# Induced attention and an ELU feed-forward: the first block attended token-major, the first batch's projected weights written in place, the first block's second layer unsplit in plain fp32, and a new order of the opening

## The chip, the cores and the metric

The kernel runs on one core of a Trainium2 chip. The metric is device time in microseconds (us); the time of a kernel is the median of its runs. The kernel before took 1676.34 us (three runs: 1674.83, 1676.34, 1676.71).

A core has five engines, each with its own instruction stream that is worked off in order: TensorE (PE in the profile; PEld is its weight load, which overlaps it), VectorE (DVE), ScalarE (ACT), GpSimd (POOL) and SyncE (SP), which here issues all DMAs. They wait for each other through semaphores. SBUF and PSUM have 128 partitions; PE writes to PSUM, in banks of 512 fp32 per partition.

## The reference

```python
def mab(q, kv):                                  # scale = 1/sqrt(128)
    s = scale * (q @ kv.transpose(0, 2, 1))
    s = s - s.max(-1, keepdims=True)
    a = np.exp(s)
    a /= a.sum(-1, keepdims=True) + 1e-09
    return a @ kv
h = mab(I, x)            # 32 inducing points attend over N tokens
y = mab(x, h)            # every token attends over the 32 rows of h
...
h = y @ w_in             # (49920, 128) @ (128, 2048)
g = np.where(h > 0.0, h, np.exp(np.minimum(h, 0.0)) - 1.0)
return g @ w_out         # (2048, 128)
```

`x` is 4 batches of 12480 tokens of 128 features, fp32. The weights arrive as fp64 and are made fp32 on the chip from their two 32-bit words.

## The kernel before

The output of the attention is never formed. For a batch, `h` (32 x 128) is multiplied by `w_in` once (`hw`, 32 x 2048), and the first layer of a block of tokens is `hw` times the softmaxed scores of the tokens. Both factors are split into two parts of the matmul's fast format fp32r, a high one and a rest; `hw` has the rows high, low, high and a row group of ones, a block's `stk` the scores high, high, low and a constant 1/32, so that one fp32r matmul of 128 rows gives the product to fp32 accuracy, plus 1.

A batch is 25 blocks (`BLOCKS`) of 512 or 480 tokens, in 7 groups (`GROUPING`). A block is worked in 8 units (`units`), a unit is 2 chunks of 128 of the 2048 hidden features. Unit n runs `ffn_in` (two matmuls into a PSUM tile `ph`, L638; exp on ACT, L646), `ffn_mid` (max and min on DVE, L652), `ffn_split` (`gh`, the part in fp32r, on ACT, L660), `ffn_low` (the rest `gl`, on POOL or DVE) and `ffn_out` (the second layer into `po`, L723). `PLAN` says how a pair of chunks does the second layer: P and D split it (six fp32r matmuls: `gh` by `wo_h`, `gh` by `wo_l`, `gl` by `wo_h`; the rest on POOL for P, on DVE for D), N does it unsplit with two fp32 matmuls, `e` by `wo_n`. P and N carry a summand of 1 in `g`, which `sum_excess` makes up for: it sums the rows of their weights on PE (L689), and L732 subtracts the sum from the output.

PE runs the second layer of a unit 3 to 5 units behind its first (`RAMP`, `LAG`). `ps_h` has 3 PSUM tiles of two banks, which the units' `ph` and, during the opening, all other products take in turn (`bank`); `ps_o` has two banks for `po`.

The opening, before unit 0, is the first batch's attention of the 32 points over its 12480 tokens (`first_batch`) and the making of the weights. Its order is written by hand in `FIRST`; a name is a step and a number: x, y the transposes of a group's tokens on PE with their copies (`COPIES` gives them to ACT or DVE), s, m scores and their maxima, b the softmax's bias of a phase, w, e, g, h the weights, their transposes, the gather on PE and its sum on DVE, then sum, share, norm, spread (`hT`, the transposed `h`), project and stack (`hw`), room (`hw`'s ones), l0 to l3 the attention of block 0 alone (`attend(b, -1)`), a0 to a3 that of the other three blocks of group 0; A to E with 0 to 3 the four parts of `w_in`, with 4 to 7 those of `w_out`: A takes the words apart (L180, L184), B makes the scale, C and D put a part together (L204, L208, L214 on DVE, L218 on POOL), E splits a part of `w_out` into `wo_h` (L253) and `wo_l` (L254) or copies it to `wo_n` (L251). A step u<n> stands for unit n: steps behind it in `FIRST` are issued after the unit's first layer. `LOADS` is the order of the loads: pieces 0 to 13 of `x`, i0 and i1 the halves of `w_in`; the parts of `w_out` follow. `BY_SCALAR` lists the parts whose scale is made mostly by ACT.

PE, DVE and ACT keep the order in which the code is written (`manual_schedule`); POOL and SP are ordered by a scheduler.

In `project_h` the four quarters of `hw` go side by side into the four partition groups of one bank, a copy and a subtraction split them, and `stack_h` places them with 12 DMAs of 32x512. The attention of block 0 (lone) computes its scores with 4 copies of `h`, transposes the 128x512 scores on DVE (L561), finds maximum, difference, exp, sum and quotient there and on ACT, transposes back (L599) and splits (L602, L604). Later batches are worked in beside the units (`side`, with the due times of `first_half` and `attend`).

Of the kernel before, what the change touches and what calls it, by code (L numbers as in the profile page):

```python
# [48 lines left out]
def kernel(  # L49
# [447 lines left out]
    def room_for_h(b):  # L497

        hw = hwp.tile([P, F], F32R, tag="hw", name=f"hw_{b}")
        if steady:  # L500
            nc.gpsimd.memset(hw[3 * Q :, :].bitcast(F32), 1.0)
# [37 lines left out]
    def lone(b, g):  # L539
        return g < 0  # L540

    def attend_scores(b, g):
# [4 lines left out]
        np_ = P if lone(b, g) else len(blocks) * Q
        ps = bank(f"ps_t_{b}_{g}")
        for j, k in enumerate(blocks):
            n = np_ // len(blocks)  # L550
            nc.tensor.matmul(  # L551
                ps[j * n : (j + 1) * n, :T],
                state[b]["hT4"][:, :n],
                block_xT(b, k),
                start=True,
                stop=True,
            )
# [37 lines left out]
    def attend_stack(b, g):  # L595
# [4 lines left out]
        if lone(b, g):  # L600
            t = home(b, 0)
            nc.scalar.copy(t[: 3 * Q], aT[: 3 * Q])  # L602
# [1 line left out]
            nc.vector.tensor_sub(low, aT[2 * Q : 3 * Q], low.bitcast(F32))  # L604
            return
# [50 lines left out]
    def ffn_split(n):  # L656
        v, how = live[n], plan(n)
        if how != "N":
            v["gh"] = ghp.tile(list(v["e"].shape), F32R, tag="gh", name=f"gh_{n}")
            nc.scalar.activation(v["gh"], v["g"], AF.Copy, bias=-1.0 if how == "D" else 0.0)  # L660
# [14 lines left out]
    def sum_excess():  # L675
        ones = ep.tile([P, TM], F32, tag="e", name="ones")[:, :P]
        ones_r = ones.bitcast(F32R)
        nc.gpsimd.memset(ones, 1.0)
        parts = []
        for cp in range(NCP):  # L680
            f = 2 * cp
            if PLAN[cp] == "P":
                i = WHERE_S[f]
                parts += [(ones_r, wo_h[:, i : i + 2, :]), (ones_r, wo_l[:, i : i + 2, :])]
            if PLAN[cp] == "N":
                parts.append((ones, wo_n[:, WHERE_N[f] : WHERE_N[f] + 2, :]))
        ps = bank("ps_excess")[:, : 2 * C]
        for i, (one, w) in enumerate(parts):
            nc.tensor.matmul(  # L689
                ps, one, w.rearrange("p c d -> p (c d)"),  # L690
                start=i == 0, stop=i == len(parts) - 1,
            )
        for dq in range(4):
            rows = slice(dq * Q, (dq + 1) * Q)
            nc.vector.tensor_reduce(
                out=excess[rows],
                in_=ps.rearrange("p (c d) -> p d c", d=C)[rows, rows, :],
                axis=AX.X, op=ALU.add,
            )
# [239 lines left out]
```

## Time and profile before

| | |
|---|---|
| median of 3 runs | 1676.34 us |
| the profiled execution | 1677.49 us |
| its span, first to last instruction | 1675.7 us |
| instructions in it | 23394 |
| mean granted TensorE clock | 0.987 |
| HBM read / written | 48.94 MB / 25.56 MB |
| first first-layer matmul (`ph`, L638) starts | 66.07 us |
| second layer of unit 8 (the first of block 1) starts | 101.89 us |

The timeline of the profile lists instructions with their start and duration in us, the engine, the line, what they write and read, a count where equal ones are merged, and in brackets how long the engine stood idle before and what ended that. An fp32 matmul shows as two passes: two of them are "x4". The granted clock of TensorE is 1.00 at full speed and 0.50 at half.

### The profile page before, as it was taken

What the parts mean: (1) busy time and instruction counts of PE and PEld (TensorE: products, weight loads), DVE (VectorE), ACT (ScalarE), POOL (GpSimd) and SP (SyncE); (2) the same over time, 40 slices, a digit from 0 to 9 for tenths busy, and PEclk for the clock granted to TensorE, in tenths of its full rate; (3) what the DMA queues carried; (4) which work ended last, traced back from release to release, by engine and by line L of the source; (5) the groups of instructions that cost most, each with busy time, mean ns of one, the idle gap of its engine ahead of it and who ended that gap; (6) DMA issues with size and microseconds to landing.
All of it is one profiled execution on the core that took longest, in us unless ns stands there. A gap on an engine that the chain in (4) does not pass through costs nothing.

```text
span 1675.7 us, 23394 instructions
## 1 busy us (share of the span) xinstructions
PE 1624.8 (97%) x7660; PEld 1214.5 (72%) x7660; DVE 1412.2 (84%) x1471; ACT 1483.1 (89%) x1718; POOL 1408.5 (84%) x740
## 2 busy tenths in 40 slices
PE   6699999999999999999999999999999999999998
PEld 4366777777776777777777677777778777777786
DVE  4898888888888888888888988888888888888886
ACT  5588999899898988988889899899889999999996
POOL 3488898887898888988888888888889989998997
PEclk9699999999999999999999999999999999999999
DMA  8253223323224243322323422321221211111111
GB/s 254 48 97 65 63 47 72 73 39 78 65 50 82 39 85 64 58 48 60 87 51 56 76 63 43 77 56 28 68 55 34 38 19 33 34 37 19 31 28 24
DMA packets 384762, 98.18 MB, mean 59 GB/s; under 512 B 364864, under 2 KB 370784, under 8 KB 384384
## 3 DMA queue, kind: packets, MB, share of 16 engines
q1 hardware_dynamic: 384640, 96.68, 28.4%
q8 instruction: 61, 1.00, 0.3%
q14 instruction: 61, 0.50, 0.1%
HBM read 48.94 MB, written 25.56 MB: 44 GB/s over the span
## 4 chain that ended last, share of the span: by engine, by line
PE 73%; DVE 9%; ACT 8%; issue 6%; DMA 2%; POOL 2%; SPq 0%; POOLq 0%; DVEq 0%; ACTq 0%
PE po L723 51%; PE ph L638 18%; ACT e L646 4%; ACT gh L660 3%; DVE e L652 3%; DMA xm<-in_x_dram 2%; PE ps_t L551 1%; DVE gl L669 1%; DVE xT L274 1%; PE ps_hh L418 1%; DVE ph L652 1%; POOL gl L673 1%; PE ps_s L327 1%; DMA out_dram<-o 1%; DVE o L731 0%
## 5 line engine op out<-in xcount | busy, mean ns | idle before, releaser
L673 POOL TENSOR_TENSOR gl<-e,gh 128x1024 fp32r<-128x1024 f32 (+1 forms) x500 | 1169.8, 2357 | 201.4 <-ACT gh L660 190.2
L646 ACT ACTIVATE e<-ph 128x1024 f32<-128x1024 f32 (+1 forms) x800 | 800.9, 1003 | 116.5 <-PE ph L638 114.9
L652 DVE SCALAR_TENSOR_TENSOR e<-ph,e 128x1024 f32<-128x1024 f32 (+1 forms) x600 | 714.3, 1192 | 184.7 <-ACT e L646 178.1
L638 PE MATMUL ph<-stk,hw 128*128 128x512 f32 (+1 forms) x1600 | 540.2, 419 | 16.2 <-DVE e L652 10.1
L723 PE MATMUL po<-gh,wo_h 128*128 128x512 f32 (+1 forms) x1400 | 546.6, 390 | 4.7 <-DVE s L561 2.5
L723 PE MATMUL po<-gh,wo_l 128*128 128x512 f32 (+1 forms) x1400 | 546.7, 390 | 0.3 <-POOL wo_l L254 0.3
L660 ACT ACTIVATE gh<-e 128x1024 fp32r<-128x1024 f32 (+1 forms) x500 | 518.8, 1038 | 25.1 <-DVE e L652 22.8
L723 PE MATMUL po<-gl,wo_h 128*128 128x512 f32 (+1 forms) x1400 | 432.0, 389 | 0.4 <-POOL gl L673 0.4
L638 PEld LDWEIGHTS ph<-stk,hw 128*128 128x128 f32 x1600 | 294.4, 189 | 164.0 <-issue 59.5
L723 PEld LDWEIGHTS po<-gh,wo_h 128*128 128x128 f32 x1400 | 263.4, 188 | 61.5 <-issue 8.2
L723 PEld LDWEIGHTS po<-gl,wo_h 128*128 128x128 f32 x1400 | 263.5, 188 | 58.5 <-POOL gl L673 1.1
L723 PEld LDWEIGHTS po<-gh,wo_l 128*128 128x128 f32 x1400 | 263.4, 188 | 53.6 <-POOL wo_l L254 0.8
L652 DVE SCALAR_TENSOR_TENSOR ph<-ph,e 128x1024 f32<-128x1024 f32 (+1 forms) x200 | 239.5, 1197 | 30.4 <-ACT e L646 28.7
L669 DVE SCALAR_TENSOR_TENSOR gl<-ph,gh 128x1024 fp32r<-128x1024 f32 (+1 forms) x200 | 237.3, 1186 | 0.1
L660 ACT ACTIVATE gh<-ph 128x1024 fp32r<-128x1024 f32 (+1 forms) x200 | 201.2, 1006 | 4.6 <-DVE ph L652 4.2
L723 PE MATMUL po<-e,wo_n 128*128 128x512 f32 (+1 forms) x400 | 183.8, 582 | 0.0
L732 POOL TENSOR_TENSOR o<-o,excess 128x512 f32<-128x512 f32 (+1 forms) x100 | 126.7, 1267 | 3.1 <-DVE o L731 3.1
L723 PEld LDWEIGHTS po<-e,wo_n 128*128 128x128 f32 x400 | 75.2, 189 | 53.2 <-issue 45.9
L731 DVE STREAM_TRANSPOSE o<-po 128x512 f32<-128x512 f32 (+1 forms) x100 | 69.1, 691 | 4.9 <-PE po L723 4.9
L274 DVE STREAM_TRANSPOSE xT<-xq 128x1024 f32<-128x1024 f32 (+2 forms) x39 | 45.5, 1166 | 0.0
L611 POOL TENSOR_TENSOR alo<-aT,ahi 128x512 fp32r<-128x512 f32 (+3 forms) x27 | 34.4, 1275 | 0.8 <-ACT ahi L609 0.8
L418 PE MATMUL ps_hh<-xm,e 128*32 128x128 f32 (+2 forms) x872 | 33.6, 295 | 0.7 <-DVE h L435 0.6
(108 smaller groups left out, 530.3 us busy)
## 6 DMA issues: line engine op xcount, KB each, us to landing
xm<-in_x_dram SPq DMA_DIRECT2D x32, 512.0 KB, 4.7
out_dram<-o SPq DMA_DIRECT2D x240, 64.0 KB, 2.0
xq<-in_x_dram SPq DMA_DIRECT2D x84, 128.0 KB, 3.0
out_dram<-o SPq DMA_DIRECT2D x160, 60.0 KB, 1.9
stk<-ahi SPq DMA_DIRECT2D x118, 64.0 KB, 2.0
xq<-in_x_dram SPq DMA_DIRECT2D x60, 120.0 KB, 2.8
stk<-ahi SPq DMA_DIRECT2D x80, 60.0 KB, 2.0
stk<-alo SPq DMA_DIRECT2D x59, 64.0 KB, 2.0
```

Of the source, the lines that this page charges most:

```text
L274: nc.vector.transpose(t, xq.rearrange("p u d -> p (u d)"))
L418: nc.tensor.matmul(ps[c * Q : (c + 1) * Q, :C], st["e", g][:np_, u * Q : (u + 1) * Q], st["xm", g, u - u % UP][:np_, u % UP, :], start=(u ...
L611: eng.tensor_sub(alo, aT, ahi.bitcast(F32))
L638: nc.tensor.matmul(ph[:, i], state[b]["hw"][:, f * P : (f + 1) * P], stacks[b, k], start=True, stop=True,)
L646: nc.scalar.activation(e, ph, AF.Exp, bias=-1.0)
L652: nc.vector.scalar_tensor_tensor(out=v["g"], in0=v["ph"], scalar=1.0, in1=v["e"], op0=ALU.max, op1=ALU.min)
L660: nc.scalar.activation(v["gh"], v["g"], AF.Copy, bias=-1.0 if how == "D" else 0.0)
L669: nc.vector.scalar_tensor_tensor(out=v["gl"], in0=v["g"], scalar=-1.0, in1=gh, op0=ALU.add, op1=ALU.subtract)
L673: nc.gpsimd.tensor_sub(v["gl"], v["e"], gh)
L723: nc.tensor.matmul(po[:, :T], w, g, start=(cp == 0 and i == 0), stop=(cp == NCP - 1 and i == len(parts) - 1),)
L731: nc.vector.transpose(o.rearrange("p u d -> p (u d)"), po[:, :T])
L732: nc.gpsimd.tensor_tensor(out=o, in0=o, in1=excess.unsqueeze(1).broadcast_to([P, U, Q]), op=ALU.subtract)
```

## The change

- **Token-major attention of block 0.** `lone_scores` multiplies each 128 tokens by `hT` (the tokens are the stationary factor), so that 4 x 32 scores of a token stand in one partition; maximum, difference, exp, sum and quotient work on 128x128 elements, the quotient writes three copies (128x384), four PE transposes bring them to 96x512 and one copy and one subtraction write `stk`.
- **`hw` in place.** `project_first` takes 96 columns of `hT4`, three copies of `h`, so that a quarter of `hw` comes out three times in three partition groups; a copy writes the 96 rows, a subtraction makes the middle 32 rows the low part. There are four such quarters with a bank each, and no DMA.
- **Block 0's second layer.** Units 0 to 7 all take two fp32 matmuls, `e` by `whole[f]`, the fp32 weights where they were put together (every second word of the raw tiles, which stay in use until then). No `gh` and no `gl` are made for them; in units 4 and 6, D in `PLAN`, POOL subtracts the 1 in place (M).
- **`sum_excess`** reads the same `whole` weights: 12 fp32 matmuls of 128 columns; four copies take the place of four reductions.
- **Ones of `hw`.** The second batch's come from the first's by a DMA in place of a memset on POOL; the third and fourth batches use the tiles of the first two again.
- **Orders.** New `FIRST`, `LOADS`, `COPIES`, `BY_SCALAR`; splits of `w_out` (E4 to E7) after units 6 to 13; the first loads of the second batch are due one block later; the switch to the later manner of working (`steady`) is tied to unit 12, where it was before.

```diff
-COPIES = "AA VA AA AA VA AA VA"
-LOADS = "0 1 2 3 i0 4 5 6 7 8 9 10 11 12 i1 13"
-BY_SCALAR = (3, 4)
+COPIES = "VA AV AA AA AA VA AA"
+LOADS = "0 1 2 i0 3 4 5 6 7 8 9 10 11 12 i1 13"
+BY_SCALAR = (3, 4, 5)
...
     def room_for_h(b):
+        if b < 2:
+            hw = hwp.tile([P, F], F32R, tag="hw", name=f"hw_{b}")
+            if b:
+                nc.sync.dma_start(
+                    hw[3 * Q :, :].bitcast(F32), state[0]["hw"][3 * Q :, :].bitcast(F32)
+                )
...
         else:
+            hw = state[b - 2]["hw"]
         state[b]["hw"] = hw
+
+    def project_first(b, c):
+        n = F // 4
+        hw = state[b]["hw"]
+        cols = slice(c * n, (c + 1) * n)
+        ps = bank(f"ps_hw_{b}_{c}")
+        nc.tensor.matmul(
+            ps[: 3 * Q, :n], state[b]["hT4"][:, : 3 * Q], win_sb[:, cols], start=True, stop=True
+        )
+        nc.scalar.copy(hw[: 3 * Q, cols], ps[: 3 * Q, :n])
+        low = hw[Q : 2 * Q, cols]
+        nc.vector.tensor_sub(low, ps[Q : 2 * Q, :n], low.bitcast(F32))
...
+    def lone_scores(b):
...
+        for i in range(n):
+            nc.tensor.matmul(
+                ps[:, i * Q : (i + 1) * Q],
+                block_xT(b, 0)[:, i * P : (i + 1) * P],
+                state[b]["hT4"][:, :Q],
...
+    def lone_exp(b):
...
+        nc.vector.tensor_reduce(out=mx, in_=ps, axis=AX.X, op=ALU.max)
...
+        nc.scalar.activation(s, s, AF.Exp, scale=SCALE)
...
+    def lone_norm(b):
...
+    def lone_stack(b):
...
+        for i in range(n):
+            nc.tensor.transpose(
+                ps[: 3 * Q, i * P : (i + 1) * P], a[:, i].rearrange("p c m -> p (c m)"), ident
+            )
+        t = home(b, 0)
+        nc.scalar.copy(t[: 3 * Q], ps[: 3 * Q, : n * P])
+        low = t[2 * Q : 3 * Q]
+        nc.vector.tensor_sub(low, ps[2 * Q : 3 * Q, : n * P], low.bitcast(F32))
...
     def plan(n):
         b, k, cp = units[n]
+        if n < NCP:
+            return "M" if PLAN[cp] == "D" else "N"
         return PLAN[cp]
...
     def ffn_low(n):
         v, how = live[n], plan(n)
-        if how == "N":
+        if how == "M":
+            nc.gpsimd.tensor_scalar(
+                out=v["e"], in0=v["e"], scalar1=-1.0, scalar2=1.0, op0=ALU.add, op1=ALU.mult
+            )
+        if how in "MN":
             return
...
+        chunks = [f for f in range(NFC) if PLAN[f // 2] != "D"]
+        ps = bank("ps_excess")[:, :C]
+        for i, f in enumerate(chunks):
+            nc.tensor.matmul(ps, ones, whole[f], start=i == 0, stop=i == len(chunks) - 1)
...
-            if how == "N":
+            if n < NCP:
+                parts.append((0, whole[f], v["e"][:, i]))
+            elif how == "N":
                 parts.append((0, wo_n[:, WHERE_N[f], :], v["e"][:, i]))
...
-        at = 0.0
+        at = 1.0 if b == 1 else 0.0
...
-        if not rest:
+        if n >= 12:
             steady.append(True)
```

The order of the opening changes throughout. The rows that follow are the program's instructions in their order, with line, operation, tile written and tiles read, and the shape.

TensorE from the transposed `h` (`ps_ht`) to the first first-layer matmul, before (`ps_t_-1` is block 0's scores, `ps_t_0` those of the three blocks after it):

```order
L471 MATMUL ps_ht_641<-sel_110,hn_637 128x128
L551 MATMUL ps_t_-1_645<-xT_0_194,hT_0_643 128x512
L482 MATMUL ps_hw_655<-win_sb,hT_0_643 32x512 x4
L551 MATMUL ps_t_0_687<-xT_0_194,hT_0_643 32x512
L551 MATMUL ps_t_0_687<-xT_1_195,hT_0_643 32x512 x2
L638 MATMUL ph_708<-stk_136,hw_639 128x512 x2
```

The same place on TensorE now (`ps_lone` is block 0's scores, `ps_lone_t` their transposes after the softmax):

```order
L473 MATMUL ps_ht_641<-sel_110,hn_637 128x128
L562 MATMUL ps_lone_647<-hT_0_643,xT_0_194 128x32 x4
L519 MATMUL ps_hw_0_665<-win_sb,hT_0_643 96x512
L621 MATMUL ps_t_0_669<-xT_0_194,hT_0_643 32x512
L621 MATMUL ps_t_0_669<-xT_1_195,hT_0_643 32x512 x2
L604 MATMUL ps_lone_t_675<-ident,lone_654 96x128 x4
L519 MATMUL ps_hw_1_682<-win_sb,hT_0_643 96x512
L519 MATMUL ps_hw_2_686<-win_sb,hT_0_643 96x512
L703 MATMUL ph_693<-stk_136,hw_576 128x512 x2
```

Three quarters of `hw` and the four transposes now stand on TensorE ahead of unit 0; the fourth quarter comes after unit 3.

TensorE at the end of block 0 now, from unit 11's first layer (`w_raw` are the whole weights, `ps_t_1` the scores of group 1):

```order
L703 MATMUL ph_838<-stk_138,hw_576 128x512 x2
L779 MATMUL po_0_745<-e_784,w_raw 128x512 x2
L703 MATMUL ph_850<-stk_138,hw_576 128x512 x2
L750 MATMUL ps_excess<-w_raw,ones 128x128 x12
L779 MATMUL po_0_745<-e_796,w_raw 128x512 x2
L621 MATMUL ps_t_1_879<-xT_2_196,hT_0_643 32x512 x2
L621 MATMUL ps_t_1_879<-xT_3_197,hT_0_643 32x512 x2
L703 MATMUL ph_890<-stk_138,hw_576 128x512 x2
```

Between two first layers there are two fp32 matmuls in every unit of the block, where six fp32r ones by `wo_h` and `wo_l` stood in seven units of eight; the lag of the second layer behind the first, and what stands at the end of the block, have not moved.

VectorE from unit 0 to the last quarter of `hw` now (`mx`, `s_0_0`, `sm` are the softmax of the three other blocks of group 0):

```order
L717 SCALAR_TENSOR_TENSOR e_696<-ph_693,e_696 128x1024
L180 TENSOR_SCALAR w_part<-w_raw 128x512
L717 SCALAR_TENSOR_TENSOR e_709<-ph_706,e_709 128x1024
L638 TENSOR_REDUCE mx_0_0_721<-s_0_0_673 96x16
L639 TENSOR_TENSOR s_0_0_673<-s_0_0_673,mx_0_0_721 96x512
L717 SCALAR_TENSOR_TENSOR e_718<-ph_715,e_718 128x1024
L651 TENSOR_REDUCE sm_0_0_731<-s_0_0_673 96x16
L657 TENSOR_SCALAR sm_0_0_731<-sm_0_0_731 96x16
L658 RECIPROCAL sm_0_0_731<-sm_0_0_731 96x16
L659 TENSOR_TENSOR s_0_0_673<-s_0_0_673,sm_0_0_731 96x512
L180 TENSOR_SCALAR w_part<-w_raw 128x512
L524 TENSOR_TENSOR hw_576<-ps_hw_3_741,hw_576 32x512
```

Before, the maximum and the difference of this softmax and the taking apart of both weight parts (L180) stood ahead of unit 0; the subtraction of a quarter of `hw` ahead of unit 3 is new.

More of the change, by code (lines that the diff above doesn't have):

```diff
@@ L234, in load_w_out @@
         return Weight(raw.rearrange("p c d -> p (c d)")), dma
+    whole = {}
     def split_w_out(s, w):
@@ L497, in room_for_h @@
     def room_for_h(b):
-        hw = hwp.tile([P, F], F32R, tag="hw", name=f"hw_{b}")
-        if steady:
-            nc.gpsimd.memset(hw[3 * Q :, :].bitcast(F32), 1.0)
-        else:
-            nc.scalar.activation(
-                hw[3 * Q :, :], largest[3 * Q :].broadcast_to([Q, F]), AF.Copy, scale=0.0, bias=1.0
-            )
+        if b < 2:
[4 more added lines that the diff above has]
+                )
+            else:
+                nc.scalar.activation(
+                    hw[3 * Q :, :], largest[3 * Q :].broadcast_to([Q, F]), AF.Copy, scale=0.0, bias=1.0
+                )
+        else:
+            hw = state[b - 2]["hw"]
         state[b]["hw"] = hw
+    def project_first(b, c):
[9 more added lines that the diff above has]
+        nc.vector.tensor_sub(low, ps[Q : 2 * Q, :n], low.bitcast(F32))
     def stack_h(b):
@@ L537, in blocks_of @@
         return range(g0 + (b == 0 and g == 0), g0 + nq)
-    def lone(b, g):
-        return g < 0
+    def lone_scores(b):
+        T = BLOCKS[0][1]
+        n = T // P
+        ps = bank(f"ps_lone_{b}")
+        for i in range(n):
[3 more added lines that the diff above has]
+                state[b]["hT4"][:, :Q],
+                start=True,
+                stop=True,
+            )
+        state[b]["lone"] = ps[:, : n * Q].rearrange("p (i m) -> p i m", m=Q)
@@ new lines, in lone_norm @@
+    def lone_norm(b):
+        s, a = state[b]["lone"]
+        n = s.shape[1]
+        sm = small.tile([P, n], F32, tag="sm1", name=f"sm1_{b}")
+        nc.vector.tensor_reduce(out=sm, in_=s, axis=AX.X, op=ALU.add)
+        nc.vector.tensor_scalar_add(sm, sm, EPS)
+        nc.vector.reciprocal(sm, sm)
+        nc.vector.tensor_tensor(
+            out=a,
+            in0=s.unsqueeze(2).broadcast_to([P, n, 3, Q]),
+            in1=sm.unsqueeze(2).unsqueeze(3).broadcast_to([P, n, 3, Q]),
+            op=ALU.mult,
+        )
+        state[b]["lone"] = a
@@ L558, in attend_scores @@
         yield 1
-        pool, tag = (ep, "e") if lone(b, g) else (once, "s2")
-        s = pool.tile([P, U, Q], F32, tag=tag, name=f"s2_{b}_{g}")
+        s = once.tile([P, U, Q], F32, tag="s2", name=f"s2_{b}_{g}")
         nc.vector.transpose(s.rearrange("p u m -> p (u m)")[:np_], ps[:np_, :T])
@@ L676, in sum_excess @@
         ones = ep.tile([P, TM], F32, tag="e", name="ones")[:, :P]
-        ones_r = ones.bitcast(F32R)
         nc.gpsimd.memset(ones, 1.0)
[L679 to L692, printed above, removed]
+        chunks = [f for f in range(NFC) if PLAN[f // 2] != "D"]
+        ps = bank("ps_excess")[:, :C]
+        for i, f in enumerate(chunks):
+            nc.tensor.matmul(ps, ones, whole[f], start=i == 0, stop=i == len(chunks) - 1)
         for dq in range(4):
             rows = slice(dq * Q, (dq + 1) * Q)
[L695 to L699, printed above, removed]
+            nc.vector.tensor_copy(excess[rows], ps[rows, rows])
     def ffn_out(n):
@@ L815, in first_batch @@
             ("sum", sum_es), ("share", share_of), ("room", room_for_h), ("norm", norm_h),
-            ("spread", spread_h), ("project", project_h), ("stack", stack_h),
+            ("spread", spread_h),
         ]:
             steps[name] = lambda f=f: list(f(b) or [])
-        for i, (_, f, _) in enumerate(attend(b, -1)):
-            steps[f"l{i}"] = lambda f=f: list(f() or [])
+        for i, f in enumerate([lone_scores, lone_exp, lone_norm, lone_stack]):
+            steps[f"l{i}"] = lambda f=f: f(b)
+        for c in range(4):
+            steps[f"p{c}"] = lambda c=c: project_first(b, c)
         for i, (_, f, _) in enumerate(attend(b, 0)):
@@ L829, in first_batch @@
                 steps[f"D{s}"] = w.finish
+                for i in range(WC):
+                    whole[(s - len(win)) * WC + i] = w.low[:, i * C : (i + 1) * C]
                 steps[f"E{s}"] = lambda w=w, s=s: split_w_out(s - len(win), w)
```

38 lines of the change are left out of this document (23 added, 15 removed).

## The prediction

> **What bounds the kernel now.** I read the page's busy shares and slices first, then the opening by stretches, then the waits of PE.
>
> ```profile
> PE 1624.8 (97%) x7660; PEld 1214.5 (72%) x7660; DVE 1412.2 (84%) x1471; ACT 1483.1 (89%) x1718; POOL 1408.5 (84%) x740
> PE   6699999999999999999999999999999999999998
> ```
>
> PE is busy 97% of the span, and every slice but the first two and the last is full. So beyond the opening nothing that the change takes from ACT, DVE or POOL can shorten the run; what counts is when PE becomes full. The stretches show when (start and end, length, then busy time of PE, PEld, DVE, ACT, POOL, the granted clock, DMA):
>
> ```profile
> 40.00:60.00 20.00, 14.68 (x156) 7.80 (x146) 15.32 (x35) 7.38 (x13) 8.43 (x11) 0.58 0.05 15
> 60.00:70.00 10.00, 2.93 (x6) 1.82 (x6) 8.91 (x17) 4.83 (x8) 3.89 (x4) 0.67 0.34 82
> 80.00:90.00 10.00, 5.25 (x15) 3.31 (x14) 9.11 (x11) 6.73 (x9) 6.54 (x5) 0.83 0.59 116
> 90.00:100.00 10.00, 9.65 (x52) 7.23 (x50) 8.24 (x11) 8.06 (x9) 10.00 (x6) 1.00 0.82 183
> ```
>
> PE is full from about 90 us on; from 60 to 70 and 80 to 90 DVE leads with 9 of 10 us, and what PE does from 40 to 70 it does at a clock near half. The waits of PE over the run, and from 110 to 1660 us alone (total, times, longest):
>
> ```profile
> PE ph L638 <- DVE e L652: 10.1, 14, 3.6
> PE ph L638 <- DVE stk L604: 6.1, 1, 6.1
> ```
> ```profile
> PE ph L638 <- DVE e L652: 4.3, 11, 0.8
> ```
>
> Only 4.3 of the 10.1 us lie in the long middle. The prize is the opening. I measure it by one mark that has the same work behind it in both kernels: the start of unit 8's second layer, with the first layers of units 0 to 13 and all of block 0 done. In the chain of waits (start, length, what):
>
> ```profile
> 101.89 1.64 PE po L723 x6
> ```
>
> **Term 1: up to `hT`.** The loads have the same bytes in nearly the same order, and the last piece of `x` still comes last. The chain of waits from there, then rows that price its new links:
>
> ```profile
> 32.42 2.37 PE ps_x L295 x14
> 34.79 1.76 PE ps_hh L418 x32
> 36.55 0.34 PE ps_pm L370 x2
> ```
> ```profile
> 33.14 0.57 ACT L304 COPY xT<-ps_x 128x448 f32<-128x448 f32 x1 [0.44 <-PE ps_x L295]
> 41.16 0.54 ACT L337 COPY s<-ps_s 128x480 f32<-128x480 f32 x1
> 42.12 0.63 DVE L344 TENSOR_REDUCE pm<-s 128x1 f32<-128x480 f32 x1
> ```
>
> Now half of the 14 transposes (y5) are done before the last piece lands (-1.2), and the gather of group 0 stands behind the bias's matmul (-1.8); in their place the transposed piece's copy, the copy of s5 behind it on ACT and its maximum on DVE come ahead (0.57 + 0.54 + 0.63 = 1.7). That is **1.3 us** earlier for the bias. From there to `hT` DVE works nearly without a gap in both orders, the same instructions. What goes is one stall:
>
> ```profile
> 48.66 1.29 POOL L218 TENSOR_TENSOR win_sb<-w_raw,w_part 128x512 f32<-128x512 f32 x1 [1.03 <-DVE w_raw L214]
> 50.01 1.80 POOL L501 MEMSET hw<- 32x2048 f32 x1
> 15.00 0.61 POOL L193 TENSOR_SCALAR w_part<-w_part 128x512 f32<-128x512 uint32 x1
> 49.98 2.11 DVE L180 TENSOR_SCALAR w_part<-w_raw 128x512 uint32<-128x512 uint32 x1 [1.41 <-POOL win_sb L218]
> 31.18 0.43 DVE L180 TENSOR_SCALAR w_part<-w_raw 128x512 uint32<-128x512 uint32 x1 [1.66 <-DMA w_raw<-in_moe_w_in_dram]
> 54.01 0.29 DVE L474 COPY hT<-ps_ht 128x128 f32<-128x128 f32 x1 [0.95 <-PE ps_ht L471]
> ```
>
> L180 waited 1.41 us for a buffer that POOL's last quarter of `w_in` held; the new order puts 3 us of other DVE work between them. Then it took 2.11 instead of 0.43 us, just while POOL wrote the second batch's ones, a memset that is now a DMA: -1.7. Against it the matmul of the exp sums now stands behind the last gather: +0.4 (my reading of the order). Term 1 is 1.3 + 1.4 + 1.7 - 0.4 = **4.0 us**, `hT` at 50.3; between 2.5 (the bias gains nothing) and 5.
>
> The Trainium skill's page "SBUF — State Buffer", section "SBUF: two separate sides", has a port pair that DVE and POOL share and that one locks for a whole instruction; the 2.11 us row agrees. By that rule the change also pays, with the two new POOL instructions of units 4 and 6; what that would cost is the second rival below.
>
> **Term 2: from `hT` to unit 0.** Before, this took 66.07 - 54.30 = 11.8 us:
>
> ```profile
> 54.35 2.08 PE L551 MATMUL ps_t_-1_645<-xT,hT 128*128 128x512 f32 x2 [0.38 <-DVE hT L474]
> 56.36 1.94 PE L482 MATMUL ps_hw<-win_sb,hT 128*32 128x512 f32 x8
> 58.07 1.93 PE L551 MATMUL ps_t<-xT,hT 128*32 128x512 f32 x6
> 66.07 2.93 PE L638 MATMUL ph<-stk,hw 128*128 128x512 f32 x6 [6.07 <-DVE stk L604]
> 27.52 0.68 PE L295 MATMUL ps_x<-ident,xm 64*128 64x64 f32 x8 [1.21 <-ACT xT L304]
> 64.68 0.62 ACT L602 CAST stk<-aT_-1_683 96x512 fp32r<-96x512 f32 x1 [3.79 <-DVE aT_-1_683 L599]
> 65.33 0.68 DVE L604 TENSOR_TENSOR stk<-aT_-1_683,stk 32x512 fp32r<-32x512 f32 x1 [0.68 <-ACT stk L602]
> ```
>
> PE was done at 60 and stood idle for 6 us while DVE did the softmax of 128x512. Now the softmax has a quarter of the elements, about 3 us on DVE and ACT (six short steps at 0.2 to 0.5), and PE needs longer than that: scores 1.0 (8 short passes; 8 transposes took 0.68 at full clock), first quarter of `hw` 1.9 (one fp32 matmul of 512 columns at half clock, as the 54.35 row), `ps_t` 1.9, transposes 0.8: 5.6. Then the copy and the subtraction, 0.62 + 0.68, 7.2 with the hops; beside them PE does two more quarters of `hw`, 3.8 us at half clock or 1.8 at full, behind 56.0. Unit 0 starts between 57.5 and 59.9; I take 58.5, so the stretch is 8.2 and the gain **3.6 us** (2.2 to 4.6). The 12 DMAs of `hw` and their landing go too.
>
> Whether the clock rises there is open, as these stretches show:
>
> ```profile
> 46.60:50.00 3.40, 3.37 (x56) 2.82 (x58) 1.81 (x7) 2.74 (x3) 1.91 (x2) 0.50 0.02 5
> 73.90:77.30 3.40, 3.01 (x8) 2.34 (x8) 2.92 (x4) 2.51 (x5) 3.40 (x3) 0.51 0.00 0
> 77.30:80.70 3.40, 3.40 (x13) 1.96 (x11) 1.84 (x2) 3.40 (x6) 3.40 (x3) 1.00 0.36 58
> ```
>
> The stretch from 73.9 brought the full clock with 3.01 us of PE work; that of the gathers, 3.37 us, did not. The Trainium skill's page "TensorE: Matmul & The Clock Gate", section "Part 1", gives full clock after some 3.4 us of sustained work. The first row speaks against it for 32-column gathers, the others agree; by the rule unit 0 would start near 57.6, 0.9 us before my value.
>
> **Term 3: block 0.** Before it took 101.89 - 66.07 = 35.8 us from unit 0 to the mark. Prices at full clock (from the chain of waits, and two groups):
>
> ```profile
> 96.08 0.47 PE ph L638 x2
> 99.50 1.06 PE L551 MATMUL ps_t<-xT,hT 128*32 128x512 f32 x8
> 103.99 1.40 PE po L723 x6
> 105.86 1.72 PE po L723 x4
> ```
> ```profile
> L673 POOL TENSOR_TENSOR gl<-e,gh 128x1024 fp32r<-128x1024 f32 (+1 forms) x500 | 1169.8, 2357 | 201.4 <-ACT gh L660 190.2
> L646 ACT ACTIVATE e<-ph 128x1024 f32<-128x1024 f32 (+1 forms) x800 | 800.9, 1003 | 116.5 <-PE ph L638 114.9
> L652 DVE SCALAR_TENSOR_TENSOR e<-ph,e 128x1024 f32<-128x1024 f32 (+1 forms) x600 | 714.3, 1192 | 184.7 <-ACT e L646 178.1
> ```
>
> An unsplit unit costs PE 1.72 instead of 1.40 us: 7 x 0.32 = 2.2 us more for the block. It rids ACT of seven copies and POOL of five subtractions of 2.36 us, and the block no longer waits for `wo_h` and `wo_l`, which are due only at the mark.
>
> First DVE leads. Unit 0 is through ACT and DVE 2.8 us after its start (0.5 + 1.0 + 1.2, a hop); unit 3's PSUM tile is the third after it, and up to the end of unit 3's `ffn_mid` DVE has three more of 1.19 (3.5), five passes over 512 elements at about 0.6 and two L180 of 0.4 (3.8), and two short ones (0.5): 7.8. So unit 5, which takes over that tile, starts at 58.5 + 10.6 = 69.1. From there PE is full: 8 first layers at 0.47 (3.8), 7 second layers at 1.72 (12.0), the sum of the weights' rows, 12 fp32 matmuls of 128 columns at a quarter of 0.86 (2.6), `ps_t_1` 1.06: 19.5, to 88.6. The bank of `ps_t_1` is the next `po`, so DVE's transposes of 0.6 with two hops come before the mark: 89.6. Together 31.1, a gain of **4.7 us**.
>
> What must stay hidden: D7's last product, needed by unit 6's second layer at 81.1. Behind unit 3, DVE has units 4 to 7 (4.8), the last steps of group 0's softmax with a wait for ACT's copy (1.9) and the putting together of parts 6 and 7 (2.9 at 0.6, 0.4 and 0.6 each): 78.7, and POOL's 1.3 (as the L218 row) gives 80.0, a slack of 1.1. POOL then has two `gl` and two `wo_l` before unit 8 can use `wo_l`, to 88.4, again 1.2 before the mark. At half clock the first 3.4 us of the full stretch would cost 1.7, two such stretches 3.4; with no wait of PE at all before 69.1 the term would gain about 3 more. So 4.7, between 1 and 8.
>
> **At no cost.** The new `COPIES` and `LOADS` act before the last load, where ACT waits 3 us in the old order; the one more scale on ACT (part 5) is done while DVE works on the softmax of block 0:
>
> ```profile
> 31.11 0.67 ACT L184 ACTIVATE w_raw<-w_raw 128x512 f32<-128x512 uint32 x1 [3.13 <-DMA w_raw<-in_moe_w_in_dram]
> ```
>
> If that cover is gone, the first costs what ACT is late, up to 1 us of term 1. The ones' DMA is ahead of nothing on SP that is due before 73 us. The second batch's first loads must now wait for the summing of the weights (86), since `w_out` stays in their buffers; they land by 90 and DVE wants them behind unit 14, about 93. If they came later, DVE would stall with the units' `ffn_mid` behind it, and PE has 5 units of work to cover that. The memsets of batches 3 and 4 were on POOL, not on the path.
>
> **The sum.** 4.0 + 3.6 + 4.7 = 12.3 us. The profiled execution took 1677.49 us, 1.15 above the median; 1677.5 - 12.3 = 1665.2, and against the median 1664.0. I forecast **1664 us**.
>
> **Rivals.**
> - *The next bound in block 0.* DVE or POOL reaches D7 or the first `wo_l` some 6 us later than I have it: term 3 gives nothing, terms 1 and 2 stay, 7.6 us, 1668.7. For it: slacks of 1.1 and 1.2 us, DVE at 9.11 of 10 us from 80 to 90 and POOL at 10 of 10 from 90 to 100; against: seven `gh` and five `gl` less.
> - *POOL holds DVE up.* The two new POOL instructions (128x1024, so twice the 0.61 us of the L193 row, 1.2 each) stop DVE's part 6 and part 7 as the memset stopped L180. That is 2.4 us on the way to D7, 1.1 of it slack: the sum is 1.3 smaller, 1665.3. For it: the 2.11 us row; against: only two of DVE's instructions there are of L180's kind.
> - *More.* All three terms at their upper ends, with PE at full clock in the opening: 17.6 us, 1658.7.
> - *No change.* The reordered opening stalls at a place I read as free (copies behind i0, weight parts behind their buffers): terms 1 and 2 are lost and half of term 3 is left, 2.3 us, 1674.
> - *Slower.* The clock stays at half through block 0. The unsplit layers and the sum then take PE double: the 19.5 us become 39, the mark comes at 109, 7 us later than before: 1683. The sign turns once over 12.3 us of full-clock work are done at half. For it: 0.58 from 40 to 60 us and 0.67 from 60 to 70; against: the 77.30 row, where PE came to full after being less busy than here.
>
> **Chances.** Forecast 0.55, next bound 0.14, POOL holds DVE up 0.10, more 0.08, no change 0.07, slower 0.06. Faster by over 0.2% (3.4 us, about what a measurement of this kernel can tell from no change) 0.87, within 0.07, slower 0.06. The range takes in the lower and upper bounds of the three terms, 5.7 to 17.6 us of gain, and with them the first three rivals: 1658.5 to 1670.5.
>
> **What would show it.** `hT` near 50.3, unit 0 near 58.5, unit 8's second layer near 89.6; L180 at 0.4 us; the clock at 1.00 from about 60 to the mark; no idle PE between unit 5 and the mark. I am wrong if PE waits for `w_raw` or `wo_l` in block 0, if the fp32 second layer by every second word takes more than 1.72 us, or if PE is not full behind the mark.

## The result and the profile after

The changed kernel takes 1663.97 us (median of 4 runs, 1663.27 to 1664.26); the kernel before, measured beside it, 1675.59 us (4 runs, 1674.41 to 1676.71). The ratio is 0.993, 95% interval 0.9913 to 0.9947: 11.6 us faster. The profiled execution took 1663.27 us, its span 1661.5. Of the runs further down, one execution of e9 took 4023.87 us at a mean granted clock of 0.40 and is left out of e9's median.

The first rows of the page: busy time of the engines, and PE's slices.

```profile
PE 1623.9 (98%) x7668; PEld 1209.1 (73%) x7668; DVE 1407.9 (85%) x1471; ACT 1478.5 (89%) x1715; POOL 1391.4 (84%) x733
PE   6899999999999999999999999999999999999998
```

PE works 0.9 us less, DVE 4, ACT 5, POOL 17 us; of all that only what lay in the opening could count. The stretches (start and end, length, busy time of PE, PEld, DVE, ACT, POOL, the granted clock, DMA):

```profile
40.00:60.00 20.00, 15.12 (x108) 7.51 (x102) 16.66 (x40) 11.10 (x16) 6.67 (x9) 0.83 0.07 15
60.00:70.00 10.00, 8.03 (x23) 4.16 (x22) 9.12 (x15) 6.00 (x9) 2.27 (x3) 1.00 0.00 0
80.00:90.00 10.00, 9.74 (x54) 6.65 (x53) 7.78 (x12) 7.27 (x10) 9.81 (x7) 1.00 0.69 127
90.00:100.00 10.00, 10.00 (x41) 7.34 (x41) 9.20 (x10) 9.46 (x11) 8.67 (x6) 1.00 0.89 161
```

From 60 to 70 PE is busy 8.03 us where it was 2.93, at the full clock; DVE still works 9.1 of 10 us there. PE's waits over the whole run (three of its rows, L717 being the `ffn_mid` that was L652), then from 110 to 1660 us:

```profile
PE ph L703 <- DVE e L717: 5.2, 12, 0.8
...
PE ph L703 <- DVE hw L524: 2.1, 2, 2.0
...
PE ph L703 <- DMA stk<-alo: 1.1, 1, 1.1
```
```profile
PE ph L703 <- DVE e L717: 4.3, 10, 0.8
```

The wait of 6.1 us for `stk` is gone and that for `e` has halved. The middle has the 4.3 us that it had. Two waits are new: for the last quarter of `hw`, and for a DMA. The marks, in the timeline:

```profile
32.75 0.18 DVE L375 TENSOR_REDUCE bias<-ps_pm 128x1 f32<-128x20 f32 x1 [0.55 <-PE ps_pm L372]
42.95 0.43 DVE L180 TENSOR_SCALAR w_part<-w_raw 128x512 uint32<-128x512 uint32 x1
45.97 0.28 DVE L476 COPY hT<-ps_ht 128x128 f32<-128x128 f32 x1
54.27 1.03 PE L703 MATMUL ph<-stk,hw 128*128 128x512 f32 x2
64.46 0.73 PE L703 MATMUL ph<-stk,hw 128*128 128x512 f32 x2 [1.97 <-DVE hw L524]
72.42 1.17 PE L703 MATMUL ph<-stk,hw 128*128 128x512 f32 x4 [1.15 <-DMA stk<-alo]
79.97 2.88 PE L750 MATMUL ps_excess<-w_raw,ones 128*128 128x128 f32 x24
86.49 0.47 PE L779 MATMUL po<-gh,wo_h 128*128 128x512 f32 x1 [0.26 <-DVE s L630]
```

`hT` is ready at 46.25 (54.30 before), unit 0 starts at 54.27 (66.07), unit 5 at 64.46, unit 8's second layer, the mark, at 86.49 (101.89). The wait of 1.15 us at 72.42 is in unit 8's first layer.

### The profile page after: what moved, and what is told of

It is laid out like the page before. It is cut to its first block, busy times and chain, and to the rows that moved or that the text cites. A ratio compares the mean times of both kernels' runs of the same rounds, so it can differ in the third digit from the quotient of the medians.

```text
span 1661.5 us, 23369 instructions
## 1 busy us (share of the span) xinstructions
PE 1623.9 (98%) x7668; PEld 1209.1 (73%) x7668; DVE 1407.9 (85%) x1471; ACT 1478.5 (89%) x1715; POOL 1391.4 (84%) x733
## 4 chain that ended last, share of the span: by engine, by line
PE 81%; DVE 7%; ACT 6%; issue 4%; DMA 1%; POOL 0%; SPq 0%; POOLq 0%; DVEq 0%; ACTq 0%
PE po L779 56%; PE ph L703 19%; ACT e L711 3%; DVE e L717 3%; ACT gh L725 2%; PE ps_t L621 2%; PE ps_s L329 1%; PE ps_hh L420 1%; DVE xT L276 1%; DMA xm<-in_x_dram 1%; DVE gl L738 1%; DVE ph L717 1%; DVE o L787 0%; PE ps_x L297 0%; ACT s L398 0%
## 5 line engine op out<-in xcount | busy, mean ns | idle before, releaser
L742 POOL TENSOR_TENSOR gl<-e,gh 128x1024 fp32r<-128x1024 f32 (+1 forms) x495 | 1156.6, 2353 | 207.5 <-ACT gh L725 200.4
L717 DVE SCALAR_TENSOR_TENSOR e<-ph,e 128x1024 f32<-128x1024 f32 (+1 forms) x602 | 716.5, 1192 | 182.9 <-ACT e L711 176.8
L779 PE MATMUL po<-gh,wo_h 128*128 128x512 f32 (+1 forms) x1386 | 539.7, 389 | 3.4 <-DVE s L630 2.1
L779 PE MATMUL po<-gh,wo_l 128*128 128x512 f32 (+1 forms) x1386 | 540.0, 390 | 0.0
L725 ACT ACTIVATE gh<-e 128x1024 fp32r<-128x1024 f32 (+1 forms) x495 | 512.9, 1036 | 21.6 <-DVE e L717 19.2
L779 PE MATMUL po<-gl,wo_h 128*128 128x512 f32 (+1 forms) x1386 | 426.8, 389 | 0.0
L779 PEld LDWEIGHTS po<-gh,wo_h 128*128 128x128 f32 x1386 | 259.8, 187 | 58.8 <-issue 7.1
L779 PEld LDWEIGHTS po<-gl,wo_h 128*128 128x128 f32 x1386 | 259.9, 188 | 54.6
L717 DVE SCALAR_TENSOR_TENSOR ph<-ph,e 128x1024 f32<-128x1024 f32 (+1 forms) x198 | 237.1, 1197 | 30.0 <-ACT e L711 28.9
L674 POOL TENSOR_TENSOR alo<-aT,ahi 128x512 fp32r<-128x512 f32 (+3 forms) x27 | 34.2, 1266 | 0.5 <-ACT ahi L672 0.5
L420 PE MATMUL ps_hh<-xm,e 128*32 128x128 f32 (+2 forms) x872 | 29.9, 275 | 2.6 <-DVE h L432 1.4
```

The lines of the kernel that those rows point to most:

```text
L420: nc.tensor.matmul(ps[c * Q : (c + 1) * Q, :C], st["e", g][:np_, u * Q : (u + 1) * Q], st["xm", g, u - u % UP][:np_, u % UP, :], start=(u ...
L674: eng.tensor_sub(alo, aT, ahi.bitcast(F32))
L717: nc.vector.scalar_tensor_tensor(out=v["g"], in0=v["ph"], scalar=1.0, in1=v["e"], op0=ALU.max, op1=ALU.min)
L742: nc.gpsimd.tensor_sub(v["gl"], v["e"], gh)
L779: nc.tensor.matmul(po[:, :T], w, g, start=(cp == 0 and i == 0), stop=(cp == NCP - 1 and i == len(parts) - 1),)
```

## The experiments

All times in this table are us in the profile of the run, the last column the median. "Landed" is the landing of the last piece of `x`, "bias" the start of the second phase's bias on DVE, "tail" the time from the mark to the start of the last second-layer matmul.

| run | landed | bias | `hT` | unit 0 | mark | tail | median |
|---|---|---|---|---|---|---|---|
| before | 32.4 | 36.91 | 54.30 | 66.07 | 101.89 | 1566.96 | 1675.59 |
| after | 29.6 | 32.75 | 46.25 | 54.27 | 86.49 | 1568.02 | 1663.97 |
| e3, before again | 31.4 | 35.44 | 52.94 | 64.72 | 100.51 | 1566.90 | 1676.06 |
| e1, after again | 30.3 | 33.58 | 47.23 | 55.36 | 87.46 | 1568.10 | 1664.28 |
| e2, after, old `LOADS` | 31.4 | 35.49 | 48.99 | 57.01 | 89.22 | 1568.19 | 1666.05 |
| e4, before, new `LOADS` | 30.2 | 34.73 | 51.68 | 63.45 | 99.25 | 1566.71 | 1674.61 |
| e5, block 0 split | 29.5 | 33.87 | 47.36 | 54.93 | 98.02 | 1568.49 | 1675.15 |
| e6, old attention of block 0 | 30.3 | 33.60 | 47.10 | 58.80 | 90.68 | 1567.82 | 1667.28 |
| e7, `hw` by DMA | 30.3 | 34.14 | 47.63 | 55.23 | 87.11 | 1568.60 | 1665.72 |
| e8, before, no memset | 31.8 | 36.36 | 52.10 | 61.89 | 97.70 | 1566.83 | 1674.12 |
| e9, after, M twice | 30.6 | 34.07 | 47.56 | 55.08 | 88.33 | 1568.25 | 1665.34 |
| e10, low part early | 30.3 | 33.70 | 47.38 | 54.68 | 87.27 | 1568.07 | 1664.46 |
| e11, quarter early too | 29.6 | 32.94 | 46.45 | 54.57 | 88.58 | 1568.02 | 1667.67 |
| e12, before, late loads | 31.3 | 35.83 | 52.76 | 64.52 | 100.30 | 1567.61 | 1677.19 |

The kernel before took 1676.33, 1676.32 and 1675.78 us beside e1 to e4, e5 to e8 and e9 to e12. Each of these groups ran on a chip of its own, so a difference between e1 and one of e5 to e12 is one between chips, on which the kernel before differs by up to 0.55 us. e3 was a single execution. All columns but the last come from one profile of each run.

**e1 and e3** are the two kernels unchanged.

> The changed kernel once more, nothing altered. Theory A (the new order of loads makes the last piece of x land early): the last transposes of x start again near 29.8 us, and the time is within 1 us of 1664. Theory B (the 2.7 us between 32.42 and 29.76 were luck of the two profiled executions): the last transposes start somewhere between 29 and 33 us.

> The kernel before once more, for a second profile. Theory A: the last transposes of x start near 32.4 us again, and unit 8's second layer near 101.9. Theory B: the last transposes start between 29 and 33 us, and the mark moves with them, to between 98.5 and 102.5 us.

On one chip, then, the gain of 11.85 us in the profiles (start of the last second layer, 1667.41 to 1655.56) falls apart into 5.71 up to `hT`, 3.65 from there to unit 0, 3.69 to the mark and -1.20 behind it. In the pair shown above the loads landed 2.8 us apart instead of 1.1, so its first part is larger.

**e2 and e4: the order of the loads.** One line, put back and put in alone:

```diff
-LOADS = "0 1 2 i0 3 4 5 6 7 8 9 10 11 12 i1 13"
+LOADS = "0 1 2 3 i0 4 5 6 7 8 9 10 11 12 i1 13"
```

> The changed kernel with the old LOADS alone (the first half of w_in behind piece 3 instead of ahead of it). Theory A: the last piece lands near 32.4 again, the bias of phase 1 comes 2 to 3 us later, and the time is 2 to 3 us above that of the changed kernel. Theory B: the landing of the last piece and the time are those of the changed kernel within 0.5 us; only what waits for the first half of w_in before 15 us moves.

> The kernel before with the new LOADS alone; its own order of the opening (transposes of group 1 first) stays. Theory A: the last piece of x lands near 29.8 us, and the time falls by 1 to 3 us. Theory B: no change beyond 0.5 us, or 0.5 us slower since group 1's second piece, which it transposes third, comes behind w_in.

The line is worth 1.77 us in the new kernel and 1.72 in the old one (ratio 0.9988, 0.9979 to 0.9997). With the old line the bias of the new kernel starts at 35.49, that of the old kernel at 35.44: in that pair all the rest of the new order gains nothing up to there. With the new line in both it does, 34.73 (e4) against 33.58 (e1), 1.15 us. The last piece of `x` is also issued earlier with the new line (at 17.03 us in e4, 17.98 in e3); why one move by one place does that isn't settled.

**e8: the ones without the memset**, `room_for_h` of the changed kernel put into the kernel before.

> The kernel before with the ones of the second batch's hw by a DMA from the first's, and the tiles used again for the third and fourth, all else old. My theory (the memset on POOL held up DVE's L180 by 1.7 us on the way to hT): L180 takes 0.4 us, hT comes 1.5 to 1.8 us earlier, time 1674.3 to 1675 where the kernel before has 1676.3. Rival (hT waits for the gathers on PE): L180 is short, hT and the time move by less than 0.5 us.

2.2 us (0.9987, 0.9979 to 0.9996). The row that took 2.11 us, in e8:

```profile
49.30 0.43 DVE L180 TENSOR_SCALAR w_part<-w_raw 128x512 uint32<-128x512 uint32 x1 [1.43 <-POOL win_sb L218]
```

The stretch while POOL wrote is gone, the wait for POOL's L218 is still there: two separate costs, as the prediction had them. From the bias to `hT` it takes 15.74 us here, 17.50 in e3 and 13.65 in e1. The remaining 2.1 us are that wait (1.43) and about the 0.63 us of a maximum over 128x480 elements that the old order does behind the bias and the new one ahead of it.

e8 changed more than the memset. From `hT` to unit 0 it takes 9.79 us, where the other four profiles of the old order have 11.76 to 11.78. VectorE's order is not the same either: one part's L204 stands ahead of the copy of `hT`, its L214 ahead of the transposition of the scores. `FIRST` is the same in both, so VectorE does not keep to the written order everywhere, as the section on the kernel before has it. The score matmul takes 1.15 instead of 2.08 us, at a clock of 0.89 instead of 0.50 (from 50 to 54 us). And the difference in block 0's softmax takes 0.69 us instead of 1.30, because POOL's L218 no longer runs beside it. The two in e3, then the difference in e8:

```profile
57.03 1.30 DVE L570 TENSOR_TENSOR s_-1_647<-s_-1_647,mx_-1_649 128x512 f32<-128x512 f32 x1
56.48 1.30 POOL L218 TENSOR_TENSOR w_raw<-w_raw,w_part 128x512 f32<-128x512 f32 x1 [4.13 <-DVE w_raw L214]
```
```profile
54.82 0.69 DVE L574 TENSOR_TENSOR s_-1_647<-s_-1_647,mx_-1_649 128x512 f32<-128x512 f32 x1
```

So the old opening lost time beside POOL at a second place, which the prediction did not see. How much of the 2.2 us is the memset's alone, e8 doesn't show.

**e5: block 0's second layer split again.** `plan` and `ffn_out` as before, and the splits E4 to E7 ahead of the units that need them:

```diff
-        if n < NCP:
-            return "M" if PLAN[cp] == "D" else "N"
...
-    p0 a0 l3 p1 p2 u0 C5 D5 u1 A6 u2 a1 u3 a2 B6 A7 p3 u4 C6 u5 a3 D6 u6 E5 u7 B7 u8 C7 D7 u9 E6
+    p0 a0 l3 p1 p2 E4 u0 C5 D5 u1 A6 u2 a1 E5 u3 a2 B6 A7 p3 u4 C6 u5 a3 D6 u6 E6 u7 B7 u8 C7 D7 E7 u9
```

> The changed kernel with block 0's second layer split again (gh, gl, wo_h and wo_l in units 0 to 7 by PLAN, no subtraction of 1 in place; the splits E4 to E7 of w_out go back between units 0 and 8). The mark is the start of unit 8's second layer, 87.5 us in the second profile of the changed kernel. My theory (the unsplit layer is what term 3 gains, 3.6 us measured): the mark 3 to 6 us later, the time 1667 to 1670. Rival (DVE sets block 0 with softmax and weights, and the unsplit layer only costs PE 2.2 us more): mark and time within 1 us of the changed kernel, or earlier.

10.9 us above e1, and nothing is left of the gain (0.9995, 0.9986 to 1.0004), far beyond what was expected. PE's waits from 50 to 100 us in e5:

```profile
PE ph L701 <- DVE e L715: 6.2, 5, 1.9
PE ph L701 <- DVE hw L524: 4.0, 2, 3.2
...
PE po L775 <- POOL wo_l L256: 0.6, 1, 0.6
```

And in e1 the rows that answer to the first two:

```profile
PE ph L703 <- DVE hw L524: 2.5, 2, 2.0
...
PE ph L703 <- DVE e L717: 0.5, 1, 0.5
```

From unit 0 to the mark e5 takes 43.1 us, the kernel before 35.8, e1 32.1. The new order puts parts of weights and of a softmax behind unit 0 that stood ahead of it; with the splits, whose copies and subtractions also want ACT, POOL and DVE, PE stands for DVE 7.2 us longer. The granted clock falls too: from unit 0 to the mark its mean is 0.84 in e5 and 1.00 in e1, and the sum of the weights' rows takes 3.4 us instead of 2.7. How much of the 11 us the waits cost and how much the clock isn't separated, and only this one placing of E4 to E7 was tried. As placed here, the new order without the unsplit layers gains next to nothing.

**e6: block 0's attention as it was**, the steps l0 to l3 as before on 128x512.

> The changed kernel with block 0's attention as before (scores with 4 copies of h, softmax of 128x512 on DVE with two transposes), all else new. My theory (term 2 is the softmax on DVE): unit 0 starts 3 to 5 us later than 55.4, and the time is 1667 to 1669. Rival (the 12 DMAs of hw, which stay away here, held unit 0): unit 0 within 1 us of 55.4, the time 1664 to 1665.

3.0 us above e1, as my theory had it, with 11.70 us from `hT` to unit 0 instead of 8.13. In e6 PE stands for `stk` again:

```profile
PE ph L713 <- DVE stk L677: 2.8, 1, 2.8
```

**e7: `hw` through 12 DMAs**, with `project_h` and `stack_h` as steps p0 and p1:

```diff
-    p0 a0 l3 p1 p2 u0 ...
+    p0 p1 a0 l3 u0 ...
```

> The changed kernel with hw made as before: four quarters side by side in one bank, one copy, one subtraction, 12 DMAs. Theory A (the DMAs are on the way): their issue and landing, some 6 us behind the subtraction, put unit 0 1 to 3 us later than 55.4, the time at 1665 to 1667.5. Theory B (in place costs PE two more full matmuls ahead of unit 0, 2.5 us in the profile, and DVE one more subtraction between units): unit 0 up to 1 us earlier and the time 1663 to 1664.5.

1.4 us above e1, within theory A's range but not for its reason: unit 0 starts at 55.23, as in e1, and nearer to `hT` (7.60 us for 8.13). PE waits 2.4 us for `hw`'s DMAs; in its place e1 has two more quarters of `hw` and the subtractions on DVE. The e7 profile is one of the faster of its five executions (1664.58 to 1666.51), with the mark 0.35 us earlier than e1's and the tail 0.5 longer, so which place costs the 1.4 us remains open.

**e9: POOL's subtraction twice.** The second one subtracts 0:

```diff
             nc.gpsimd.tensor_scalar(
                 out=v["e"], in0=v["e"], scalar1=-1.0, scalar2=1.0, op0=ALU.add, op1=ALU.mult
             )
+            nc.gpsimd.tensor_scalar(
+                out=v["e"], in0=v["e"], scalar1=0.0, scalar2=1.0, op0=ALU.add, op1=ALU.mult
+            )
```

> The changed kernel with POOL's subtraction of the 1 in units 4 and 6 followed by a second one of the same shape that subtracts 0, so two more POOL instructions of 128x1024 (1.04 us each by the changed kernel's profile). Theory A (they lie beside DVE work that is not held, and part 7 has slack): within 0.3 us of the changed kernel, 1663.9 to 1664.6. Rival (POOL holds DVE up while they run, the second rival of the prediction): DVE's instructions under them stretch from 0.43 to over 1 us and the time is 1 to 2 us more, 1665.3 to 1666.3.

1.1 us above e1 in the median, the low end of what the rival gave; the two differ in chip as well. In e9, DVE and POOL (L733 is the second subtraction):

```profile
69.83 1.49 DVE L674 TENSOR_TENSOR alo<-aT,ahi 96x512 fp32r<-96x512 f32 x1 [0.69 <-ACT ahi L672]
75.95 1.16 DVE L208 TENSOR_SCALAR w_raw<-w_raw 128x512 uint32<-128x512 uint32 x1
...
69.74 1.04 POOL L733 TENSOR_SCALAR e<-e 128x1024 f32<-128x1024 f32 x1
75.41 1.42 POOL L733 TENSOR_SCALAR e<-e 128x1024 f32<-128x1024 f32 x1
```

The same two DVE instructions in the changed kernel, with the subtraction that is nearest to the first:

```profile
67.94 1.04 POOL L730 TENSOR_SCALAR e<-e 128x1024 f32<-128x1024 f32 x1 [2.85 <-DVE e L717]
69.15 0.69 DVE L674 TENSOR_TENSOR alo<-aT,ahi 96x512 fp32r<-96x512 f32 x1 [0.68 <-ACT ahi L672]
74.47 0.43 DVE L208 TENSOR_SCALAR w_raw<-w_raw 128x512 uint32<-128x512 uint32 x1
```

Where they run at once, DVE's instruction takes 0.7 to 0.8 us more. In the changed kernel POOL is done at 68.98 and L674 starts at 69.15: it escapes by 0.2 us. The Trainium skill's page "SBUF — State Buffer", section "SBUF: two separate sides", says that a DVE operation with two SBUF inputs, or in a two-port mode, and a GpSimd operation that reads SBUF shut each other out of the ports that they share. L674 has two SBUF inputs and agrees. L208 has one, and no run here shows whether it works in a two-port mode. The stretching is shown; that it makes the 1.1 us is not, since the clock differs too: in e9 it was 0.66 from 65 to 70 us, where e1 has 1.00 from 60 to 70.

**e10 and e11: taking the two new waits away.** In e10 the transpose of group 0's scores and the copy on ACT (a3) come ahead of unit 5, the low part and its DMAs (a4) behind it; e11 also moves the last quarter of `hw` (p3) and part 7's taking apart (A7):

```diff
-u2 a1 u3 a2 B6 A7 p3 u4 C6 u5 a3 D6 u6
+u2 a1 u3 a2 B6 A7 p3 u4 a3 u5 a4 C6 D6 u6
```
```diff
+u2 a1 p3 u3 a2 B6 u4 A7 a3 u5 a4 C6 D6 u6
```

> The changed kernel with group 0's transposed scores and their copy moved ahead of unit 5, their low part and the DMAs behind unit 5, and the steps of weight part 6 behind those. Theory A (the 1.16 us that PE stood in unit 8's first layer came from the late low part, about 1.7 us earlier now; PE is full from unit 5 on otherwise): the wait is gone, the mark 1.0 to 1.2 us earlier, 1662.8 to 1663.3. Rival (DVE is the bound of the stretch, and another wait, for part 6 or for a PSUM tile behind DVE, takes its place): 1664.0 to 1664.6.

> As the run before, and the last quarter of hw moved from behind unit 3 to behind unit 2, weight part 7's taking apart behind unit 4. Theory A (unit 5 stood 1.96 us for the subtraction of that quarter, queued on DVE behind a softmax step and part 7): unit 5 starts about 1.4 us earlier, and with the low part early too the mark comes about 2 us earlier than in the changed kernel: 1661.8 to 1662.8. Rival (unit 8 then waits for the low part again, since the softmax on DVE stands behind the quarter's subtraction): no better than the run before, 1662.8 to 1663.6.

Neither is faster than the changed kernel: e10 0.2 us above e1, which is what its rival gave, e11 3.4. In e10 the wait for the DMA is gone, and this stands in its place:

```profile
72.50 0.73 PE L706 MATMUL ph<-stk,hw 128*128 128x512 f32 x2 [0.96 <-DVE e L720]
...
68.19 1.52 DVE L204 SCALAR_TENSOR_TENSOR w_part<-w_raw,w_part 128x512 uint32<-128x512 uint32 x1
...
67.75 1.42 POOL L733 TENSOR_SCALAR e<-e 128x1024 f32<-128x1024 f32 x1 [2.38 <-DVE e L720]
```

L204 now runs beside POOL's subtraction and takes 1.52 us where 0.68 is usual; the units' `ffn_mid` behind it come late. In e11 there is one idle time of DVE more:

```profile
61.76 0.68 DVE L524 TENSOR_TENSOR hw<-ps_hw,hw 32x512 fp32r<-32x512 f32 x1 [1.17 <-ACT hw L522]
...
73.82 0.73 PE L706 MATMUL ph<-stk,hw 128*128 128x512 f32 x2 [2.51 <-DVE e L720]
```

Both theories of e11 gave less than 1663.6, so both failed: the copy of the quarter on ACT comes behind two exps, DVE stands for it, and PE's largest wait, 2.51 us, is longer than either of the two taken away. The other four executions of e11 took 1667.57 to 1667.98, 2.3 to 2.7 us above the profiled one; what is late there was not seen.

**e12: the second batch's loads a block later**, alone in the kernel before:

```diff
-        at = 0.0
+        at = 1.0 if b == 1 else 0.0
```

> The kernel before with nothing but the second batch's first loads due one block later, as in the changed kernel. Theory A (the 1.1 us that the changed kernel loses behind the mark come from the second batch's steps of the first half coming later and closer together): the time from the mark to the last second layer is 1567.7 to 1568.2 where it was 1566.9, and the run is 1.0 us slower than before, 1677.0 to 1677.6. Rival (they come from the splits of the output weights standing behind unit 9, or from the DMA of the ones): 1566.7 to 1567.1, and the time is before's, 1676.0 to 1676.6.

The tail is 1567.61, 0.7 of the 1.2 us longer; the median rises by 1.4 us, a difference that the interval (0.9998 to 1.0016) doesn't set apart from none. PE's waits from 100 to 450 us, in e12:

```profile
PE ph L638 <- DVE e L652: 1.4, 3, 0.8
...
PE ps_t L551 <- DVE h L428: 0.5, 1, 0.5
```

From 100 to 450 in the kernel before, then from 86 to 450 in the changed one:

```profile
PE ph L638 <- DVE e L652: 1.1, 2, 0.7
```
```profile
PE ph L703 <- DVE e L717: 1.6, 4, 0.8
...
PE ps_t L621 <- DVE h L430: 0.5, 1, 0.5
```

The wait of `ps_t` for `h` comes with the later loads, in e12 as in the changed kernel, and so does one more wait for `e` (the changed kernel has two more). What makes the other 0.5 us is open.

## Why the prediction was right, and where it was not

The forecast of 1664.0 and the measured 1663.97 agree more closely than the steps do, and that is luck: between e3 and e1, term 1 gave 1.7 us more than forecast, term 3 1.0 less and the work behind the mark 1.2 less. The last column has the new `LOADS` in both kernels.

| | predicted | shown pair | e3 to e1 | e4 to e1 |
|---|---|---|---|---|
| term 1, up to `hT` | 4.0 | 8.05 | 5.71 | 4.45 |
| term 2, to unit 0 | 3.6 | 3.78 | 3.65 | 3.64 |
| term 3, to the mark | 4.7 | 3.60 | 3.69 | 3.70 |
| behind the mark | 0 | -1.06 | -1.20 | -1.39 |
| sum | 12.3 | 14.4 | 11.85 | 10.40 |

- **Term 1 was too small, and its upper end of 5 missed.** The step that failed stands in two sentences: "The loads have the same bytes in nearly the same order", and, among the edits at no cost, that `LOADS` acts ahead of the last load. The last piece lands 1.1 us earlier, and the line gives 1.7 us in either kernel (e2, e4), where I had 0. With the line the same in both kernels the term is close to its 4.0: 3.95 us with the old one (e3 to e2) and 4.45 with the new one (e4 to e1). Its parts were less sure: the 1.3 us up to the bias came as 1.15 with the new line and not at all with the old one.
- **L180's two costs were right in kind** (e8): its stretch under the memset gone, 2.11 to 0.43 us, and its wait for POOL gone in the changed kernel. From the bias to `hT` I had 2.7 us; e3 to e1 shows 3.85. There DVE did not work "nearly without a gap in both orders": it stood 3.65 us in e3 and 1.51 in e1. Besides L180's 1.41 the 0.95 us for which the copy of `hT` waited for PE are gone, filled with L204 and L208.
- **Term 2 was right**: 8.2 us predicted, 8.02 and 8.13 measured, and e6 gives back 3.6 us of it. In the new order its cause is block 0's attention on fewer elements; the DMAs of `hw`, which I listed with it, gave nothing at unit 0 (e7). But the 11.8 us that it starts from were not all softmax: with the old attention e8 has 9.79.
- **Term 3 was near in size up to unit 5** (10.2 us after unit 0 for 10.6, beside an `excess` of 2.72 us for 2.6), though not for the reason given: unit 5 was let go by the subtraction of the last quarter of `hw`, when unit 3's `ffn_mid`, which I had it wait for, only began (64.44). It was wrong in "From there PE is full": unit 8's first layer stood 1.15 us for the DMA of the low part. I priced D7 and `wo_l` as what must stay hidden and left out the chain of group 0's softmax, which ends in DMAs. D7 was done on POOL at 77.0, 22.7 us behind unit 0 where I had 21.5; unit 6's second layer started 0.8 us later, so the slack was smaller than my 1.1.
- **The terms are not separate.** Term 3 bears 4.7 us in the sum, but without the unsplit layers 11 us go in e5, where the clock was lower as well. A price worked out edit by edit doesn't see that one edit makes the room in which another's work is put.
- **Behind the mark I had no loss.** I weighed the later loads by whether they land in time; they did, and their steps stood elsewhere among the units' (e12, 0.7 of 1.2 us).
- **The rivals.** The next bound did not come: neither D7 nor `wo_l` was waited for. That POOL's two new instructions hold DVE up did not happen in the changed kernel, by 0.2 us, but DVE's instructions do stretch beside POOL's in e9 and e10, and in e10 new waits of 0.96 and 0.40 us for `e` stand where one of 1.16 for the DMA was. The clock was 1.00 through block 0, so the slower case did not come either.

## What to carry to other kernels

In an opening that one engine leads, take elements and instructions off that engine: moving them about only moved the wait (e10, e11), while a softmax of a quarter of the size gave 3 us. A DMA order whose bytes don't change is not free of price; measure it alone, it is one line. And when an edit frees engines and another fills them, try the second without the first before adding their prices.

## What the runs showed of the hardware

The granted clock in the opening is not set by the kernel alone. The stretch from `hT` to unit 0, in which PE does the scores and the quarters of `hw`, in the changed kernel and in e10, whose instructions on PE are the same up to there:

```profile
46.25:54.27 8.02, 7.96 (x25) 3.54 (x25) 5.74 (x14) 2.95 (x6) 2.05 (x3) 0.57 0.00 1
```
```profile
47.38:54.68 7.30, 5.63 (x25) 2.17 (x25) 5.49 (x14) 3.27 (x6) 2.05 (x3) 1.00 0.00 1
```

At 0.57 PE is busy 7.96 us, at 1.00 5.63, and the stretch takes 8.02 against 7.30 us, a difference of 0.7 where the prediction gave 0.9 for it. And an fp32 matmul whose stationary weights are every second word cost no more than a dense one: the two second-layer matmuls of an unsplit unit of block 0 took 1.72 us in the chain of waits, the price that the prediction took from the dense `wo_n`:

```profile
73.59 1.72 PE po L779 x4
```
